# Attention forward: the loads of V are issued from another engine's DMA queue

## The chip, the cores and the metric

The kernel runs on one core of one Trainium2 chip. The metric is the device time of one execution in microseconds (us). A core has a matrix engine (PE; its weight loads are shown as PEld), a vector engine (DVE), a scalar engine (ACT), a general engine (POOL) and a synchronising engine (SP) that here does nothing but issue DMAs. Sixteen DMA engines move data between the device memory and the on-chip buffer.

## The reference

Plain softmax attention over 16 x 32 = 512 heads, each with 192 queries, 1024 keys and a head width of 128, all in bfloat16:

```python
B, H, Sq, Sk, D = 16, 32, 192, 1024, 128

def reference(q, k, v):
    scale = q.shape[-1] ** -0.5
    scores = jnp.einsum("bhqd,bhkd->bhqk", q, k) * scale
    p = _softmax(scores, axis=-1)
    return jnp.einsum("bhqk,bhkd->bhqd", p, v)
```

## The kernel before

**Heads, pairs, units.** Two heads make a pair, and their 2 x 192 query rows are cut into three units of 128 rows: `A` is 128 rows of the first head, `B` 128 rows of the second, and `S` the remaining 64 rows of each. Two pairs, that is four heads with six units (`A0 B0 A1 B1 S0 S1`), make one period; the three order strings at the top of the file say in which order each engine works on a period's units, and a prime in them means "of the period before". Sixteen heads (`G=16`) make a group of 24 units and four periods (`UPG = 24`); there are 32 groups (`NGR`).

**What is done to a unit.** PE multiplies q by the transposed K into PSUM (`qk`, buffer `s_ps`). DVE scales the scores, copies them to the on-chip buffer `ss` and finds the row's extreme (L332). ACT takes the exponential with the row sum (L373), or, for the units called shifted, POOL subtracts the maximum (L207) and ACT takes the exponential later. PE transposes the result (`tr`, buffer `pt_ps`), ACT evacuates that to `pt_sb` (`evac`, L382 and L384), and PE multiplies it by V (`pv`, buffer `o_ps`). DVE divides by the row sums into `ob` (L357). On PE the `pv` products run one period behind the `qk` products, that of `B1` two periods behind, so the last `pv` of a group is the first `pv` in the second period of the next group.

**Loads and stores.** All DMAs are issued by SP, in one order. K and q are loaded by transposing DMAs into `kt` and `qt` (L141, L145), V by a plain DMA into `vs` (L152), in runs of 2048 bytes. Each of the three buffers has two slots (`NS=2`), each holding a whole group, so group g goes into the slot of group g - 2. Group 0 comes in three pieces (`FIRST`), group 1 whole. After that, SP goes through the groups: for each g it loads K and q of g + 2 once all `qk` of g are done (semaphore `s_qk`, L161), loads V of g + 2 once all `pv` of g are done (`s_pv`, L164), and then stores the outputs of g once they are complete (`s_on`, L169). A DMA issue that finds its queue full holds SP until there is room.

**Who waits for V.** PE waits for the V of a group at the group's first `pv` (L313, semaphore `svl`), for q at its first `qk` (L257) and for K right after (L266). ACT's program is one list (`ACT_ORDER`, L20, run at L387):

```python
ACT_ORDER = "exp:B0 exp:A1 ev:A0 ev:B0 exp:S0 ev:A1 exp:S1 ev:B1 ev:S0 ev:S1"
```

Of the kernel before, what the change touches and what calls it, by code (L numbers as in the profile page):

```python
# [12 lines left out]
UNITS = ("A0", "B0", "A1", "B1", "S0", "S1")  # L13
# [9 lines left out]
def _order(text, periods):  # L23
    ops = [(w.split(":")[0], w.split(":")[1].rstrip("'"), w.count("'")) for w in text.split()]
    for p in range(periods + max(back for _, _, back in ops)):
        for op, name, back in ops:
            if 0 <= p - back < periods:
                if name in UNITS:
                    yield op, 6 * (p - back) + UNITS.index(name)
                else:  # L30
                    yield op, 2 * (p - back) + int(name)


def _attention_kernel(nc, q, k, v, out, G=16, NS=2, NSS=5, NX=4, NPT=5,
                      FIRST=((0, 2), (2, 8), (8, 16)), LAST=((0, 4), (4, 6), (6, 7), (7, 8))):
# [5 lines left out]
    NGR = NH // G  # L41
    PPG = G // 2
    UPG = 3 * PPG
    NU = NGR * UPG
    KT_TILES = SK // 128
# [7 lines left out]
    vf = v.rearrange("b h s d -> (b h) s d")  # L53
    of = out.rearrange("b h s d -> (b h) s d")

    def shifted(u):
        return UNITS[u % 6] in SHIFTED
# [12 lines left out]
    with ExitStack() as es:  # L70
        def sb(name, shape, dt):
            return es.enter_context(nc.sbuf_tensor(name, shape, dt))
# [4 lines left out]
        def sem(name):  # L77
            return es.enter_context(nc.semaphore(name))
# [3 lines left out]
        vs = sb("vs", [128, NS, G, KT_TILES, 128], BF16)  # L82
# [15 lines left out]
        svl = [sem("svl%d" % i) for i in range(NS)]  # L98
        sf = [sem("sf%d" % i) for i in range(len(FIRST))]
        sfv = [sem("sfv%d" % i) for i in range(len(FIRST))]  # L100
# [7 lines left out]
        s_pv = sem("s_pv")  # L108
# [5 lines left out]
        def unit_info(u):  # L114
            name = UNITS[u % 6]
            pr = 2 * (u // 6) + int(name[1])
            return pr, "ABS".index(name[0]), pr // PPG, pr % PPG
# [3 lines left out]
        def words(t):  # L121
            return t.rearrange("p t q -> p (t q)").bitcast(F32)
# [10 lines left out]
        def pair_units(pr):  # L133
            return [u for u in range(6 * (pr // 2), 6 * (pr // 2) + 6) if unit_info(u)[0] == pr]

        @block.sync
        def _(e):
            def load_kq(g, a, b, sems):
                s = g % NS
                h0 = g * G  # L140
                e.dma_start_transpose(  # L141
                    kt[:, s, :, a * 128:b * 128],
                    kf[h0 + a:h0 + b].rearrange("g (p t) d -> (g p) (t d)", t=KT_TILES),
                ).then_inc(sems[0], 16)
                e.dma_start_transpose(  # L145
                    qt[:, s, a * SQ:b * SQ],
                    qf[h0 + a:h0 + b].rearrange("g r d -> (g r) d"),
                ).then_inc(sems[1], 16)

            def load_v(g, a, b, sm):  # L150
                h0 = g * G
                e.dma_start(  # L152
                    vs[:, g % NS, a:b],
                    vf[h0 + a:h0 + b].rearrange("g (p t) d -> p g t d", t=KT_TILES),
                ).then_inc(sm, 16)

            def loads(g):
                s = g % NS
                last_u = (g - NS + 1) * UPG - 1
                if g >= NS:  # L160
                    e.wait_ge(s_qk, last_u + 1)  # L161
                load_kq(g, 0, G, (sxk[s], sxq[s]))
                if g >= NS:
                    e.wait_ge(s_pv, last_u + 1)  # L164
                load_v(g, 0, G, svl[s])

            def stores(g, a, b):
                so = g % NSO
                e.wait_ge(s_on, g * PPG + b)  # L169
                e.dma_start(  # L170
                    of[g * G + 2 * a:g * G + 2 * b].rearrange("h r d -> (h r) d").rearrange(
                        "(n p) d -> p n d", p=128),
                    ob[:, so, a:b].rearrange("p pg y d -> p (pg y) d"),
                ).then_inc(sst[so], 16)

            n = len(FIRST)
            for i in range(n):
                load_kq(0, *FIRST[i], (sf[i], sf[i]))
                if i > 0:
                    for i2 in range(i if i > 1 else 0, i + 1):  # L180
                        load_v(0, *FIRST[i2], sfv[i2])
            for g in range(1, min(NS, NGR)):
                loads(g)
            for g in range(NGR):
                if g + NS < NGR:
                    loads(g + NS)
                for a, b in (LAST if g == NGR - 1 else ((0, PPG),)):
                    stores(g, a, b)
            for so in range(min(NSO, NGR)):
                n_uses = len(range(so, NGR, NSO))  # L190
                if so == (NGR - 1) % NSO:
                    n_uses += len(LAST) - 1
                e.wait_ge(sst[so], 16 * n_uses)
# [23 lines left out]
        def _(pe):  # L217
# [19 lines left out]
            def qk(u):  # L237
# [13 lines left out]
                if g == 0:  # L251
                    for i, (h, _) in enumerate(FIRST):
                        if h <= b and i not in seen_kq:
                            seen_kq.add(i)
                            pe.wait_ge(sf[i], 32)
                elif u % UPG == 0:
                    pe.wait_ge(sxq[s], load_cnt(g))  # L257
# [27 lines left out]
            def pv(u):  # L285
# [14 lines left out]
                for t in range(KT_TILES):  # L300
                    first = t == 0
                    last = t == KT_TILES - 1
                    for at, rows, x in tiles:
                        w = PTS[:, t, rows]
                        pe.ldweights(w, tile_position=at)  # L305
                        if first and at[1] == 0:
                            if g == 0:
                                for i, (h, _) in enumerate(FIRST):
                                    if h <= b and i not in seen_v:
                                        seen_v.add(i)  # L310
                                        pe.wait_ge(sfv[i], 16)
                            elif u % UPG == 0:
                                pe.wait_ge(svl[s], load_cnt(g))  # L313
                            if k3 == 0 and pr >= 2:
                                pe.wait_ge(s_on, pr - 1)
                        ins = product(O[rows, sl, :], w, vs[:, s, x, t, :], at, first, last)
                        if with_rs:
                            ins = product(O[rows, 3, sl: sl + 1], w, ones[:, 0:1], at, False, last)
# [49 lines left out]
        @block.scalar  # L368
        def _(act):
            def exp_first(u):  # L370
                act.wait_ge(s_max, u + 1)
                pr, k3, g, pg = unit_info(u)
                act.activation(  # L373
                    x_sb[:, u % NX, :], ss[:, u % NSS, :], ACT_FN.Exp,
                    bias=nb[:, u % NSS: u % NSS + 1], scale=-1.0,
                    accum_out=rs[:, pr % NRS, O_SLOT[k3]: O_SLOT[k3] + 1],
                ).then_inc(s_xa, 1)

            def evac(u):
                act.wait_ge(s_tr, u + 1)  # L380
                if shifted(u):
                    act.activation(pt_sb[:, u % NPT], pt_ps[u % 2][:], ACT_FN.Exp, scale=-1.0).then_inc(s_ev, 1)  # L382
                else:
                    act.activation(words(pt_sb[:, u % NPT]), words(pt_ps[u % 2][:]), ACT_FN.Copy).then_inc(s_ev, 1)  # L384

            do = {"exp": exp_first, "ev": evac}
            for op, u in _order(ACT_ORDER, NU // 6):  # L387
                do[op](u)


def bass_standalone__mha_softmax__near_ridge_kernel(
    nc: bass.Bass,
    q: bass.AP,
    k: bass.AP,
    v: bass.AP,
    out: bass.AP,
):
    _attention_kernel(nc, q, k, v, out)
# [28 lines left out]
```

## Time and profile before

| what | value |
|---|---|
| median of 3 runs | 1204.29 us (1203.57 to 1207.56) |
| profiled execution, its time | 1201.59 us |
| its span, first to last instruction | 1199.9 us |
| granted clock of PE | 0.984 |
| busy PE / DVE / ACT / POOL | 94% / 91% / 90% / 40% |
| PE waits for q | 32.7 us in 12 waits |
| PE waits for V | 29.6 us in 22 waits |
| moved by DMA | 321.25 MB, 268 GB/s on average |
| packets of the DMA queue that the program's own transfers use | 789712, 318.78 MB |
| packets of the instruction queue (queue 8) | 132, 2.16 MB |

The span is the time from the first to the last instruction of the one profiled execution; the run that it was taken from took 1201.59 us, and the median of the timed runs is 2.7 us above that. The page gives each engine's busy time, the span cut into 40 slices with the busy share of each engine and of the DMA engines in tenths (9 is 90% or more), and the chain of work that ended last. A time "to landing" is from a DMA's issue to the arrival of its data. In SP's timeline the length of a row is how long SP was held by that issue, not how long the data took.

The transfers of one group as the trace has them (us from the start of the span; group 15 is in the middle of the run):

| transfer | issued | SP held for | landed |
|---|---|---|---|
| K of group 15 | 536.10 | 25.91 | 566.0 |
| q of group 15 | 562.06 | 4.58 | 568.7 |
| V of group 15 | 566.68 | 0.58 | 581.8 |
| outputs of group 13 | 567.31 | 4.63 | 584.4 |

For the same group, the last `qk` product of group 13, whose slots it takes, ends at 535.9, and the last `pv` product of group 13 at 546.8.

### The profile page before, as it was taken

What the parts mean: (1) busy time and instruction counts of PE and PEld (TensorE: products, weight loads), DVE (VectorE), ACT (ScalarE), POOL (GpSimd) and SP (SyncE); (2) the same over time, 40 slices, a digit from 0 to 9 for tenths busy, and PEclk for the clock granted to TensorE, in tenths of its full rate; (3) what the DMA queues carried; (4) which work ended last, traced back from release to release, by engine and by line L of the source; (5) the groups of instructions that cost most, each with busy time, mean ns of one, the idle gap of its engine ahead of it and who ended that gap; (6) DMA issues with size and microseconds to landing.
All of it is one profiled execution on the core that took longest, in us unless ns stands there. A gap on an engine that the chain in (4) does not pass through costs nothing.

```text
span 1199.9 us, 38792 instructions
## 1 busy us (share of the span) xinstructions
PE 1130.4 (94%) x18432; PEld 849.9 (71%) x15360; DVE 1089.1 (91%) x2304; ACT 1082.9 (90%) x1793; POOL 485.3 (40%) x262
## 2 busy tenths in 40 slices
PE   5699999999999999999999999999999999999998
PEld 3477777777777777677776777777777777777766
DVE  5589899989998999899999999989999899989987
ACT  4689899989998999899998999989999899989988
POOL 2234344434343434344443443434444344334432
PEclk9899999999999999999999999999999999999999
DMA  9999999999999999999999999999999999999991
GB/s 233 244 280 276 284 283 259 262 293 280 284 269 243 282 284 282 278 269 258 287 288 273 286 259 269 290 283 276 270 251 281 289 281 288 259 252 294 284 273 32
DMA packets 789882, 321.25 MB, mean 268 GB/s; under 512 B 724176, under 2 KB 724176, under 8 KB 789712
## 3 DMA queue, kind: packets, MB, share of 16 engines
q1 hardware_dynamic: 789712, 318.78, 112.2%
q8 instruction: 132, 2.16, 0.7%
q14 instruction: 38, 0.31, 0.1%
HBM read 134.22 MB, written 25.17 MB: 133 GB/s over the span
## 4 chain that ended last, share of the span: by engine, by line
PE 62%; DMA 29%; SPq 8%; ACT 2%; issue 0%; DVE 0%
DMA vs<-in_v_dram 28%; PE o_ps L220 22%; PE pt_ps L220 20%; PE s_ps L220 19%; SPq L141 4%; SPq L145 3%; ACT x_sb L373 1%; DMA qt<-in_q_dram 1%; ACT pt_sb L384 0%; ACT pt_sb L382 0%; SPq L152 0%; DVE ob L357 0%; DVE rinv L355 0%
## 5 line engine op out<-in xcount | busy, mean ns | idle before, releaser
L332 DVE TENSOR_SCALAR_CACHE_REDUCE ss<-s_ps 128x1024 f32<-128x1024 f32 x768 | 920.4, 1220 | 94.3 <-PE s_ps L220 76.4
L207 POOL TENSOR_TENSOR x_sb<-ss,nb 128x1024 bf16<-128x1024 f32 x256 | 484.6, 1893 | 702.6 <-DVE ss L332 683.3
L305 PEld LDWEIGHTS <-pt_sb 128*128 128x128 bf16 (+1 forms) x8192 | 443.8, 104 | 232.8 <-issue 135.1
L373 ACT ACTIVATE x_sb<-ss,nb 128x1024 bf16<-128x1024 f32 x512 | 585.3, 1145 | 12.6 <-DVE ss L332 12.6
L220 PE MATMUL o_ps<-vs,pt_sb 128*128 128x128 bf16 (+1 forms) x8192 | 498.1, 219 | 31.8 <-DMA vs<-in_v_dram 29.6
L220 PE MATMUL s_ps<-kt,qt 128*128 128x512 bf16 (+1 forms) x2048 | 468.7, 387 | 33.2 <-DMA qt<-in_q_dram 32.7
L220 PE MATMUL pt_ps<-ident,x_sb 128*128 128x128 bf16 x6144 | 454.5, 221 | 1.3 <-ACT pt_sb L382 1.3
L279 PEld LDWEIGHTS <-x_sb 128*128 128x128 bf16 x6144 | 369.2, 98 | 62.4 <-issue 62.1
L384 ACT ACTIVATE pt_sb<-pt_ps 128x512 f32<-128x512 f32 x512 | 306.0, 598 | 79.3 <-PE pt_ps L220 79.0
L382 ACT ACTIVATE pt_sb<-pt_ps 128x1024 bf16<-128x1024 bf16 x256 | 260.1, 1016 | 19.7 <-PE pt_ps L220 19.6
L220 PE MATMUL o_ps<-ones,pt_sb 128*128 128x1 bf16 x2048 | 190.0, 166 | 0.0
L357 DVE TENSOR_TENSOR ob<-o_ps,rinv 128x384 bf16<-128x384 f32 x256 | 142.7, 557 | 8.8
L263 PEld LDWEIGHTS <-qt 128*128 128x128 bf16 (+1 forms) x1024 | 79.8, 104 | 51.4 <-DMA qt<-in_q_dram 28.3
L373 ACT ACTIVATION_READ_ACCUMULATOR x_sb<-ss,nb 128x1 f32 x512 | 100.7, 197 | 0.0
L332 DVE DVE_READ_ACCUMULATOR ss<-s_ps 128x1 f32 x768 | 63.6, 83 | 0.0
L355 DVE RECIPROCAL rinv<-o_ps 128x1 f32<-128x1 f32 x256 | 41.6, 163 | 4.2 <-PE o_ps L220 4.2
L345 DVE RECIPROCAL rinv<-rs 128x2 f32<-128x2 f32 x256 | 40.9, 160 | 1.1 <-ACT x_sb L373 1.1
L373 ACT ACT_TABLE_LOAD x1 | 1.3, 1283 | 0.8 <-PEq L412 0.8
L199 POOL TENSOR_SCALAR_AFFINE_SELECT ident<-ones 128x128 bf16<-128x128 bf16 x1 | 0.3, 292 | 0.1
L197 POOL MEMSET ones<- 128x128 bf16 x1 | 0.2, 204 | 0.3 <-POOLq L412 0.3
L412 POOL MEMSET const-float32-0.0<- 128x1 f32 x1 | 0.1, 99 | 0.3 <-issue 0.3
L412 POOL MEMSET const-bfloat16-1.0<- 128x1 bf16 x1 | 0.1, 102 | 0.0
(2 smaller groups left out, 0.2 us busy)
## 6 DMA issues: line engine op xcount, KB each, us to landing
vs<-in_v_dram SPq DMA_DIRECT2D x31, 4096.0 KB, 15.2
out_dram<-ob SPq DMA_DIRECT2D x31, 768.0 KB, 17.1
vs<-in_v_dram SPq DMA_DIRECT2D x1, 2048.0 KB, 10.2
vs<-in_v_dram SPq DMA_DIRECT2D x1, 1536.0 KB, 8.8
kt<-in_k_dram SPq DMA_TRANSPOSE x34, 30.4
qt<-in_q_dram SPq DMA_TRANSPOSE x34, 6.1
vs<-in_v_dram SPq DMA_DIRECT2D x1, 512.0 KB, 4.6
out_dram<-ob SPq DMA_DIRECT2D x1, 384.0 KB, 3.2
```

Source lines behind the costliest of these rows:

```text
L141: e.dma_start_transpose(kt[:, s, :, a * 128:b * 128], kf[h0 + a:h0 + b].rearrange("g (p t) d -> (g p) (t d)", t=KT_TILES),).then_inc(sems[ ...
L207: gp.tensor_tensor(x_sb[:, u % NX, :], ss[:, u % NSS, :], nb[:, u % NSS: u % NSS + 1].to_broadcast([128, SK]), ALU.subtract,).then_inc(s_x ...
L220: return pe.add_instruction(mybir.InstMatmult(name=nc.get_next_instruction_name(), engine=mybir.EngineType.PE, ins=[pe.lower_ap(x), pe.low ...
L263: pe.ldweights(w, tile_position=at)
L279: pe.ldweights(w, is_transpose=True, tile_position=(0, 0))
L305: pe.ldweights(w, tile_position=at)
L332: dve.tensor_scalar(ss[:, u % NSS, :], s_ps[u % 2][:].rearrange("p t k -> p (t k)"), -scale, None, ALU.mult, ALU.min, accum_out=nb[:, u % ...
L355: dve.reciprocal(rinv[:, pr % 2, sel], o_ps[pr % 2][:, 3, sel]).then_inc(s_ri, 1)
L357: dve.tensor_tensor(ob[:, so, pg], o_ps[pr % 2][:, 0:3, :], rinv[:, pr % 2, 0:3].unsqueeze(2).to_broadcast([128, 3, 128]), ALU.mult,).then ...
L373: act.activation(x_sb[:, u % NX, :], ss[:, u % NSS, :], ACT_FN.Exp, bias=nb[:, u % NSS: u % NSS + 1], scale=-1.0, accum_out=rs[:, pr % NRS ...
L382: act.activation(pt_sb[:, u % NPT], pt_ps[u % 2][:], ACT_FN.Exp, scale=-1.0).then_inc(s_ev, 1)
L384: act.activation(words(pt_sb[:, u % NPT]), words(pt_ps[u % 2][:]), ACT_FN.Copy).then_inc(s_ev, 1)
```

## The change

Of the V loads, those of groups 0 and 1 stay at SP. Those of groups 2 to 31 are issued by ACT, one DMA of 16 heads for each group as before. ACT issues the load of group g after its evacuation of unit `A1` in the first period of group g - 1, and waits before it until all `pv` of group g - 2 are done, the same count that SP waited for. SP's list for those groups is then K, q, store. Nothing else changes; the helper `load_v` moves out of SP's program and takes the engine as an argument.

```diff
+        def load_v(e, g, a, b, sm):
+            h0 = g * G
+            e.dma_start(
+                vs[:, g % NS, a:b],
+                vf[h0 + a:h0 + b].rearrange("g (p t) d -> p g t d", t=KT_TILES),
+            ).then_inc(sm, 16)
+
         @block.sync
         def _(e):
...
             def loads(g):
                 s = g % NS
                 last_u = (g - NS + 1) * UPG - 1
                 if g >= NS:
                     e.wait_ge(s_qk, last_u + 1)
                 load_kq(g, 0, G, (sxk[s], sxq[s]))
-                if g >= NS:
-                    e.wait_ge(s_pv, last_u + 1)
-                load_v(g, 0, G, svl[s])
+                if g < NS:
+                    load_v(e, g, 0, G, svl[s])
...
             for op, u in _order(ACT_ORDER, NU // 6):
                 do[op](u)
+                g = u // UPG - 1 + NS
+                if op == "ev" and u % UPG == UNITS.index("A1") and NS <= g < NGR:
+                    act.wait_ge(s_pv, (g - NS + 1) * UPG)
+                    load_v(act, g, 0, G, svl[g % NS])
```

More of the change, by code (lines that the diff above doesn't have):

```diff
@@ L148, in load_kq @@
                 ).then_inc(sems[1], 16)
[L150 to L155, printed above, removed]
             def loads(g):
@@ L180, in _ @@
                     for i2 in range(i if i > 1 else 0, i + 1):
-                        load_v(0, *FIRST[i2], sfv[i2])
+                        load_v(e, 0, *FIRST[i2], sfv[i2])
             for g in range(1, min(NS, NGR)):
```

## The prediction, made before the changed kernel was run

> **What bounds the kernel now.** I read the page first (the DMA line, the issues, the chain), then SP's timeline, then rates in short windows.
>
> ```profile
> DMA  9999999999999999999999999999999999999991
> DMA vs<-in_v_dram 28%; PE o_ps L220 22%; PE pt_ps L220 20%; PE s_ps L220 19%; SPq L141 4%; SPq L145 3%; ACT x_sb L373 1%; DMA qt<-in_q_dram 1%; ACT pt_sb L384 0%; ACT pt_sb L382 0%; SPq L152 0%; DVE ob L357 0%; DVE rinv L355 0%
> vs<-in_v_dram SPq DMA_DIRECT2D x31, 4096.0 KB, 15.2
> out_dram<-ob SPq DMA_DIRECT2D x31, 768.0 KB, 17.1
> ```
>
> The DMA engines are at 9 tenths or more in every slice but the last. The largest link of the chain of waits is the landing of V, not compute. SP's own timeline, start, length and instruction, shows why V comes when it does:
>
> ```profile
> 530.87 0.58 SPq L152 DMA_DIRECT2D vs<-in_v_dram  x1
> 531.49 4.56 SPq L170 DMA_DIRECT2D out_dram<-ob  x1
> 536.10 25.91 SPq L141 DMA_TRANSPOSE kt<-in_k_dram  x1
> 562.06 4.58 SPq L145 DMA_TRANSPOSE qt<-in_q_dram  x1
> 566.68 0.58 SPq L152 DMA_DIRECT2D vs<-in_v_dram  x1
> 567.31 4.63 SPq L170 DMA_DIRECT2D out_dram<-ob  x1
> 571.98 27.49 SPq L141 DMA_TRANSPOSE kt<-in_k_dram  x1
> ```
>
> Each row starts where the one above ends (562.06 + 4.58 = 566.64, next 566.68): SP is never held by a semaphore here, only by a queue that is full. From the V issue at 129.68 to that at 1149.38 lie 28 groups, so a group takes 36.42 us. Compute alone is faster. In the chain in order of time the sixteen transposes of one period of four heads come back every 8.64 us, so a group of 16 heads needs 34.56:
>
> ```profile
> 79.30 1.00 PE pt_ps L220 x16
> 87.94 1.00 PE pt_ps L220 x16
> 96.57 1.00 PE pt_ps L220 x16
> 105.21 1.00 PE pt_ps L220 x16
> ```
>
> The difference, 1.86 us a group, is what PE waits for loads: for V 29.6 us in 22 waits and for q 32.7 in 12. Windows (length, busy time of PE, PEld, DVE, ACT and POOL, clock, DMA share, GB/s) give the rates. The first is K alone, the second V alone, the third a hole in the K transposes:
>
> ```profile
> 558.00:560.00 2.00, 2.00 (x48) 1.53 (x43) 1.97 (x4) 1.76 (x3) 0.91 (x1) 1.00 1.28 290
> 570.00:572.00 2.00, 2.00 (x32) 1.38 (x19) 2.00 (x5) 2.00 (x4) 0.00 (x0) 1.00 1.05 404
> 589.20:590.40 1.20, 1.20 (x24) 1.00 (x15) 1.20 (x3) 1.20 (x3) 0.00 (x0) 1.00 0.18 7
> ```
>
> Per group: K 4.19 MB at 290 GB/s is 14.5 us, q 0.79 MB 2.7, V 4.19 MB at 404 is 10.4, and the store 0.79 MB 2.7 at K's rate: 30.3 us. The other 6.1 of 36.42 are such holes and the seams between transfers. Most holes follow an instruction fetch (queue 8, 132 packets of 16 KB): while one DMA engine carries that packet, the transposes of all sixteen stop. So the kernel is paced by DMA work.
>
> **The change, part by part.**
>
> *SP loses 30 V issues* (groups 2 to 31; four stay). They took 0.58 us each, 17 us in all, but SP spends its time blocked on a full queue, so this is worth 0 on the path.
>
> *ACT gains 30 issues and 30 waits.* Each stands after the evacuation of A1 in a group's first period. That evacuation needs its transposes, which PE runs right behind the last probabilities-times-V product of the group before; the semaphore has reached its count by then, so I cost the wait at 0. Behind the issue stand the exp of S1 and then evacuations that PE waits for. The issue is put at 0.58 us, SP's row. It delays ACT, which is busy 3.76 or 4.00 of each 4 us in steady state, about 1.0 us free a group; the 1.86 us of DMA cover stand over that. If both covers were gone: 30 x 0.58 = 17 us. Bounds: 0 to 4.6 us each (a direct transfer issued behind a backlog, the store rows above); I take 0.58, the same instruction, hence 0 on the path.
>
> *V's transfer moves.* Now it is issued some 20 us after it could be: group 13's last V product ends at 546.8, and V(15), which takes its slot, is issued at 566.68. Afterwards it starts about 1 to 2 us after that product and shares the engines with K(g) of the same group. V was late and becomes early; K and q, which shared with nobody, become late. That is no exchange at par, since q opens a group's compute and V is wanted only 11 us later (q product first done at 537.5, V product first done at 548.1).
>
> Following it from the start: K(2) is issued at 58.70 and q(2) lands at 95.0, V(2) behind it at 106.9. Afterwards V(2) is issued at about 76 (group 0's last V product ends at 74.3) and its 10.4 to 11.9 us go ahead of the rest of K(2) and q(2), so q(2) lands at about 106. From there each period carries the same list, K, q, V, store, and stays saturated. At the end V(31) landed last, at 1164.9, and q(31) at 1152.9; now q(31) is last, at about 1164.9, a delay of 12.0. What follows q(31) was 1199.9 - 1152.9 = 47.0 us, in it about 1 us of waiting for V, which goes. Sum: +12 - 1 = +11 us. I also stepped through it with the pieces K 18.3, q 3.3, V 11.3, store 3.5 (the 30.3 with the 6.1 spread over them) and compute of 34.56: this gives 1200.1 for the kernel before (trace 1199.9) and 1210.8 with V and K sharing evenly.
>
> The Trainium skill (DMA: Bandwidth & Descriptors, "Queues, rings and completion order") says that an engine takes turns between queues packet by packet. V's 2048-byte packets take 84 ns in the trace and K's 256-byte ones 14 (1134 a us over 16), so by that rule V would get six sevenths, and the same stepping gives 1212.3. Nothing in the sum rests on it.
>
> *What two queues do to the rate* the trace does not show in bulk. From below: the holes fill and the period falls to compute's 34.56, -1.86 x 29 = -54 us. From above: each group gets another pair of seams like those seen where transposes end and V starts (0.87 us lost) and where the store ends and K starts (0.75), 1.6 x 29 = +47. The nearest row is the fetch, a plain packet from another queue amid transposes: it takes 960 ns there against 1053 within V, so passing costs it nothing, and within a V stretch it costs the others 0.11 us. I take 0.1 a group, +3 us.
>
> The Trainium skill (same page, "Issuing engines are not separate DMA queues") says that a second issuing engine saves only the issue time, since all run on the same 16 DMA engines. The rows agree that issue is not what is short. By it the rate term would be 0 and the sum +11.
>
> Sum: +11 + 3 = +14 on the profiled span of 1199.9 (its run took 1201.59). The median shown is 1204.29, 2.7 above that run; I add the same 14: **1218**.
>
> **The rivals.**
>
> *The holes fill (faster).* Place: K's holes. A fetch that falls into K costs 0.97 us of the next 1.5, one of queue 14 0.66: 83 and 25 of them, 97 us, 3.2 a group. If V flows on the idle engines during them, half of it is 1.6 x 29 = 46, less the 11: 1204 - 35 = 1169; capped by compute it is 1204 - 54 + 11 = 1161. It decides from 0.38 us a group on (11 / 29). For it: sixteen engines do stand idle. Against: at 562.80 an 8 KB packet of queue 14 came while the transposes were about to stop, and took 1679 ns instead of 309, ending with the hole; a plain packet behind stuck transposes seems to be stuck too.
>
> *New seams (slower by more).* The 1.6 us a group above: 1204 + 11 + 47 = 1262. For it: transposes stop on all engines when one is late, and V makes them uneven. Against: the fetch's own time. A milder form: V gets little, a quarter of the engines, lands after it is wanted, and the stepping gives +24: 1228.
>
> *ACT is held.* If the issue takes the store's 4.6 us: 4.6 - 1.86 - 1.0 = 1.7 a group, 49, and the first q(2) 7 later: 1260. Against: V's issue at SP stayed at 0.58 with K and q queued ahead of it.
>
> *Nothing moves.* The one-time delay is recovered because the list is no longer saturated: 1204. Against: the DMA line.
>
> **How the numbers follow.** Forecast 0.48 (own range 1208 to 1228), holes fill 0.20, new seams or a small share 0.17, ACT held 0.09, nothing 0.06. The range 1175 to 1270 leaves out half of the faster case and the tail of the slow ones, about 0.17. A measurement tells 0.3%, 3.6 us, from no change. Faster is the first rival with a bit of the fourth: 0.21; same 0.07; slower 0.72.
>
> **What would show it.** Right: DMA still at 9 in every slice; V issued some 20 us earlier against its product and PE's waits for V gone; waits for q and K in its place, with q(2) landing near 106 and the last q near 1165; a period still within 0.3 us of 36.4; the issue at ACT near 0.6 us. Wrong: windows in which K and V together move clearly more, or less, than the 30.3 us account says; holes that V fills; ACT idle behind its issue; a period near 34.6 or above 37.

## The result, and the profile after

The changed kernel takes 1281.05 us (1273.52 to 1283.61) against 1203.99, a ratio of 1.062 [1.057, 1.067]. The forecast was 1218 with a range up to 1270: the direction was right, the time lies 11 us above the range. The profiled execution has a span of 1281.9 against 1199.9, 82.0 us more.

The page of the changed kernel: the DMA engines by slices, the chain of waits by line, and the DMA issues with their time to landing.

```profile
DMA  9999999999999999999999999999999999999962
PE o_ps L219 24%; PE s_ps L219 23%; PE pt_ps L219 22%; DMA qt<-in_q_dram 22%; SPq L148 6%; DMA vs<-in_v_dram 1%; SPq L152 1%; ACT x_sb L372 0%; SPq L138 0%; ACT pt_sb L383 0%; ACT pt_sb L381 0%; DVE ob L356 0%; DVE rinv L354 0%
vs<-in_v_dram ACTq DMA_DIRECT2D x30, 4096.0 KB, 23.3
kt<-in_k_dram SPq DMA_TRANSPOSE x34, 36.6
qt<-in_q_dram SPq DMA_TRANSPOSE x34, 8.5
```

The engines have packets in flight for 9 tenths of nearly every slice, as before, but that counts packets that stand still too: they move 251 GB/s on average against 268. V, 28% of the chain before, is 1% now; q, 1% before, is 22%. K now lands 36.6 us after its issue (30.4 before), q after 8.5 (6.1), V after 23.3 (15.2). What PE waited for, in us, times and longest, in the changed kernel:

```profile
PE s_ps L219 <- DMA qt<-in_q_dram: 123.9, 31, 10.1
PE o_ps L219 <- DMA vs<-in_v_dram: 1.0, 1, 1.0
```

The waits for V (29.6) are gone, those for q have grown from 32.7 to 123.9. ACT's own price is not among them. Its timeline around one V issue:

```profile
587.54 0.59 ACT L383 ACTIVATE pt_sb<-pt_ps 128x512 f32<-128x512 f32 x1
588.02 1.15 ACT L372 ACTIVATE x_sb<-ss,nb 128x1024 bf16<-128x1024 f32 x1
588.35 0.38 ACTq L138 DMA_DIRECT2D vs<-in_v_dram  x1
```

The issue takes 0.38 us and lies under an exponential of 1.15.

**Where the 82 us are.** I take the time at which the first product of a group with q is done. For group 2 it moved from 98.0 to 109.7: +11.7, once. From group 2 to group 31 a group takes 38.87 us in place of 36.40: 29 x 2.47 = +71.6. From there to the end 44.9 in place of 46.2: -1.3. Together 82.0. (The product times that the text before the result gives for groups 0, 13 and 14 are one product too late: the last products of group 13 end at 534.5 and 545.2, about 1.5 us earlier, and the last V product of group 0 at 71.3, 3 us earlier. The distances that were used, 11 us and some 20, stand.)

So the price is a rate. It is not PE's clock: the granted clock is 0.953 against 0.984, but PE's waits for q are 4.0 us a group (123.9 in 31), and with the 34.56 of compute they make 38.6 of the 38.87. Windows of the changed kernel (length, busy times, clock, DMA share, GB/s): K alone; K and V together; a hole after an instruction fetch while V and K alternate; the start of V:

```profile
586.00:588.00 2.00, 2.00 (x37) 1.65 (x26) 2.00 (x4) 2.00 (x4) 0.30 (x1) 1.00 1.28 290
602.00:604.00 2.00, 2.00 (x43) 1.41 (x35) 1.97 (x5) 2.00 (x5) 1.57 (x1) 1.00 1.07 388
605.80:606.80 1.00, 1.00 (x23) 0.90 (x14) 0.93 (x4) 1.00 (x3) 0.82 (x1) 1.00 1.34 46
595.00:596.50 1.50, 1.50 (x29) 1.15 (x17) 1.50 (x3) 1.50 (x4) 0.00 (x0) 1.00 0.70 49
```

Together the two queues move 388 GB/s, no more than V alone (404 before), and between 604 and 605 us of the span the trace has 175 packets of V and 175 of K, as many of one as of the other. A packet of V has 2048 bytes and one of K 256, so in this stretch V gets eight ninths of what is moved. The Trainium skill (DMA: Bandwidth & Descriptors, "Queues, rings and completion order") has engines take turns by packets; these equal counts agree.

The loss lies in the holes. I counted packets in slices of 0.1 us, called 1134 small packets or 196 of V a us full speed, and summed what is missing, for groups 5 to 29:

| kernel | us a group | lost a group |
|---|---|---|
| before | 36.44 | 6.13 |
| changed | 38.83 | 8.52 |

Both differ by 2.39. That has to be so, since each group moves the same packets and the period less the loss is 30.3 in both; what the count adds is the place of the loss. In the kernel before, holes with a fetch cost 3.81 us a group, all of them among K, q and outputs; within V, counted as holes, they cost 0.01. In the changed kernel they cost 2.67 there and 2.55 while V and K alternate, 5.22 in all. A 16 KB fetch during V cost 0.11 of the next 1.5 us before, and costs 0.80 now. The seams, where one kind of transfer gives way to another (transposes to V; in the changed kernel also V back to transposes), cost 0.97 before and 2.0 now. So of the 2.39, fetches account for 1.41 and seams for 1.03.

### The profile page after: what moved, and what is told of

The parts are those of the page before. It is cut to its first block, busy times and chain, and to the rows that moved or that the text cites. A ratio compares the mean times of both kernels' runs of the same rounds, so it can differ in the third digit from the quotient of the medians.

```text
span 1281.9 us, 38792 instructions
## 1 busy us (share of the span) xinstructions
PE 1151.8 (90%) x18432; PEld 863.2 (67%) x15360; DVE 1088.6 (85%) x2304; ACT 1084.4 (85%) x1793; POOL 485.3 (38%) x262
## 4 chain that ended last, share of the span: by engine, by line
PE 69%; DMA 23%; SPq 7%; ACT 1%; issue 0%; DVE 0%
PE o_ps L219 24%; PE s_ps L219 23%; PE pt_ps L219 22%; DMA qt<-in_q_dram 22%; SPq L148 6%; DMA vs<-in_v_dram 1%; SPq L152 1%; ACT x_sb L372 0%; SPq L138 0%; ACT pt_sb L383 0%; ACT pt_sb L381 0%; DVE ob L356 0%; DVE rinv L354 0%
## 5 line engine op out<-in xcount | busy, mean ns | idle before, releaser
L304 PEld LDWEIGHTS <-pt_sb 128*128 128x128 bf16 (+1 forms) x8192 | 452.2, 105 | 208.4 <-issue 112.7
L219 PE MATMUL s_ps<-kt,qt 128*128 128x512 bf16 (+1 forms) x2048 | 479.0, 392 | 124.5 <-DMA qt<-in_q_dram 123.9
L219 PE MATMUL o_ps<-vs,pt_sb 128*128 128x128 bf16 (+1 forms) x8192 | 507.1, 220 | 1.1 <-DMA vs<-in_v_dram 1.0
L219 PE MATMUL pt_ps<-ident,x_sb 128*128 128x128 bf16 x6144 | 459.6, 222 | 1.3 <-ACT pt_sb L381 1.3
L219 PE MATMUL o_ps<-ones,pt_sb 128*128 128x1 bf16 x2048 | 200.1, 170 | 0.0
## 6 DMA issues: line engine op xcount, KB each, us to landing
vs<-in_v_dram ACTq DMA_DIRECT2D x30, 4096.0 KB, 23.3
kt<-in_k_dram SPq DMA_TRANSPOSE x34, 36.6
```

What stands on the lines that cost most here:

```text
L219: return pe.add_instruction(mybir.InstMatmult(name=nc.get_next_instruction_name(), engine=mybir.EngineType.PE, ins=[pe.lower_ap(x), pe.low ...
```

## The experiments

Times are compared with the kernel before on the same chip, whose median was 1199 to 1204.

**V early, but in one queue.** K in two parts, V between them, all at SP; and as control the same cut with V behind q:

```diff
...
+                load_k(g, 0, 12, sxk[s])
+                e.wait_ge(s_pv, last_u + 1)
                 load_v(g, 0, G, svl[s])
+                load_k(g, 12, G, sxk[s])
+                load_q(g, 0, G, sxq[s])
...
```

> V is back in SP's queue, put where it now arrives: after the K of 12 heads, ahead of the K of the last 4 and of q. The order of the data is that of the changed kernel, the packets of V and K do not alternate. If alternating packets cost the 2.4 us a group (38.83 against 36.44), the period returns to 36.4 to 36.9 and only the one-time delay of q stays: 1204 + 11 to 25, 1215 to 1230. If the order costs it (K of the next group waits for its slot with nothing but a store to cover it), the period stays at 38.5 or more and the time at 1270 to 1285.

> Control for the run above: K in two transposes of 12 and 4 heads, V behind q at SP as in the kernel before. Both theories: within 5 us of 1204. Above 1215 the cut of K itself has a price, which is then taken off the run above.

Measured: 1266.41, 1.051 [1.047, 1.056]; control 1213.50, 1.007 [1.004, 1.010]. SP's timeline of the first:

```profile
527.78 14.20 SPq L144 DMA_TRANSPOSE kt<-in_k_dram  x1
542.02 1.54 SPq L163 DMA_DIRECT2D vs<-in_v_dram  x1
543.61 15.92 SPq L144 DMA_TRANSPOSE kt<-in_k_dram  x1
559.57 4.18 SPq L152 DMA_TRANSPOSE qt<-in_q_dram  x1
563.80 0.58 SPq L185 DMA_DIRECT2D out_dram<-ob  x1
```

Much of such a price comes without any second queue. A group takes 38.10 us against 36.79 in the control: 1.31 for V's place alone, more than half of the 2.47. SP is hardly held by K's slot: the rows follow one another, and over the whole run the issue of K waits 7.0 us in all, 15.5 in the changed kernel. So the theory that K waits for its slot falls; lost time a group is 7.82 against 6.55, and the seam where V gives way to K, which the control does not have, accounts for 1.40. That does not divide the 2.47 of the changed kernel: there V's packets alternate with K's, and its own count has 1.03 on seams and 1.41 on fetches. What this pair shows is that a V in the middle of K has a price of this size without any second queue.

**V in two pieces in one queue.** K in 10, 3 and 3 heads, half of V in each gap.

```diff
...
+                load_k(g, 0, 10, sxk[s])
+                e.wait_ge(s_pv, last_u + 1)
+                load_v(g, 0, 8, svl[s])
+                load_k(g, 10, 13, sxk[s])
+                load_v(g, 8, G, svl[s])
+                load_k(g, 13, G, sxk[s])
+                load_q(g, 0, G, sxq[s])
...
```

> As the run with V between two parts of K in SP's queue, but K in 10, 3 and 3 heads and V in two halves between them: one more place where V follows K and one more where K follows V. If each such pair of seams costs some 1.3 us a group, and each cut of K 0.4, the period rises from 38.1 to 39.5 to 40 and the time from 1266 to 1305 to 1320. If it was the early place of V, not the seams: V is no earlier than there, 1266 to 1280.

Measured 1336.44, 1.114 [1.112, 1.116]; 40.53 us a group. A second cut adds 2.4 us, more than the seam theory's 1.3 and the 0.4 for a cut of K, so its size was too small and its direction right. V's bytes did not change and the place of its first half only by two heads of K; what changed most is the number of seams.

**Half of V on each queue.**

```diff
...
-                    load_v(act, g, 0, G, svl[g % NS])
+                    load_v(act, g, 0, G // 2, svl[g % NS])
...
```

with the other 8 heads from SP behind q.

> 8 heads of V from ACT as in the changed kernel, the other 8 from SP behind q as before. Alternating packets: half of the 2.4 us a group, period 37.6, and half of the one-time delay: 1204 + 35 + 6 = 1245, 1235 to 1255. Order (K waiting for its slot with too little cover): 2 MB of V, 5.2 us, lie between q and the next K again, so nearly all of it goes: 1210 to 1220.

Measured 1321.51, 1.096 [1.092, 1.099]: worse than all of V on ACT, against both theories, 40.42 us a group. Half the alternating packets did not halve the loss. What did grow is the number of places where V enters: once among K and once behind q, with 9.83 us lost a group. This fits seams, not packets.

**More instruction fetches**, in the kernel before and in the changed one: 32 empty instructions after each subtraction on POOL.

```diff
...
                 ).then_inc(s_xp, 1)
+                for _ in range(32):
+                    gp.engine_nop()
...
```

> The kernel before with 32 empty instructions after each subtraction on POOL, which has time for them: 256 more instructions a group, one instruction fetch of 16 KB more a group, 32 in all. Fetches stop all transposes for some 1.26 us and hardly touch V alone: two thirds of them fall into K, 32 x 0.84 = 27, 1225 to 1235. If the holes only happen to stand beside fetches, or POOL's instructions matter in another way: 1200 to 1210.

> The same 32 empty instructions in the changed kernel. If V that alternates with K no longer shelters a fetch, each costs its 1.2 us wherever it falls: 32 x 1.2 = 38, 1281 + 38 = 1319, 1312 to 1326, so more than the 27 of the kernel before. If V shelters as before: 1281 + 27 = 1308.

Measured: 1211.38, 1.010 [1.007, 1.013], and 1295.04, 1.080 [1.078, 1.082]. The instructions came as 64 more packets of 8 KB on queue 14, not as 32 of 16 KB. More fetches do slow the kernel, about 12 us in the kernel before and, taking 1.080 less 1.062, about 21 in the changed one. The second is larger as expected, but 1.062 is known to half a per cent only, so 15 to 28 us is possible against 9 to 15: that V shelters fetches less when it alternates with K rests on the counts in the trace, and this pair does not settle it.

**V from ACT, but later.** The unit named in the condition moves the issue: the third period after A1, its end after S1, the second period after A1.

```diff
-                if op == "ev" and u % UPG == UNITS.index("A1") and NS <= g < NGR:
+                if op == "ev" and u % UPG == 12 + UNITS.index("A1") and NS <= g < NGR:
```

> V stays in ACT's queue, but is issued in the third period of a group instead of the first, some 17 us later, when most of K and q of that group have passed. If alternating packets cost the time, little is left to alternate with: 1204 to 1225, period below 37.2. If the second queue as such is slow, or costs ACT time, nothing is gained: 1275 to 1290. If the order with an early V was the cost, V behind q gives 1204 to 1215.

> V from ACT some 3.5 us later than in the third-period run, after the evacuation of S1, without a wait for q. If the price of the second queue lies in V entering among K and q of its own group, V now comes behind them in nearly every group: 1195 to 1215, with less scatter than 1199 to 1244. If V now runs into K of the next group instead and splits it: 1230 to 1290.

> V from ACT in the second period, halfway between the changed kernel (1281) and the run with the third period (1229). By seams and alternating packets V still enters in the middle of K or just ahead of q, so as many seams as in the changed kernel, and q is late by all of V: 1265 to 1300. If the loss shrinks in step with how late V enters: 1250 to 1260.

Measured: third period 1229.05, but from 1199.14 to 1243.60, too scattered for an interval; its end 1299.75, 1.081 [1.078, 1.085]; second period 1190.51, 0.990 [0.983, 0.997]. None of the three medians lies in a range that I expected, and the price does not fall steadily the later V comes. At the end of the third period V is issued about 2 us before K of the next group and runs into it. There it also comes too late, and PE waits for it 98.2 us (29.6 in the kernel before, 1.0 in the changed one), so this time is not the price of a split K alone:

```profile
PE o_ps L219 <- DMA vs<-in_v_dram: 98.2, 30, 4.6
```

In the second period it meets the end of q: 5.49 us lost a group, less than the 6.13 of the kernel before, and the seam in front of V, 0.97 there, down to 0.4. So the second queue as such is not slow.

Two neighbours of it, after B1 and after S1 of the second period:

> V from ACT in the second period, after the evacuation of B1, some 1.7 us later than the run that took 1190 against 1200. If V is best where it enters with the end of q, so that neither K nor q is cut and V starts without a hole (lost per group 5.5 us there, 6.1 in the kernel before, 8.5 in the changed one): fewer packets of q alternate with V, 0.98 to 0.99 of the kernel before, 1176 to 1190. If that run was a lucky phase: 1200 to 1250.

> The same after the evacuation of S1, some 3.5 us later than the first. By the end-of-q theory V now follows q or just meets its last packets: 0.975 to 0.99, 1170 to 1188. If the gain needs V to overlap q's end, part of it is lost again and some groups fall into the bad case seen in the third period (V just ahead of a late q): 1195 to 1230.

Measured 1200.26, 1.003 [1.000, 1.005], and 1202.96, 1.003 [1.000, 1.005]. Neither expected gain came. The trace of the first says why: of its 29 steps from group 2 on, 17 are 34.5 us, the time of compute alone, and five are 39.6 to 41.5 (steps are from one group's first product with q to the next's). The first of these, from SP's and then ACT's timeline:

```profile
212.75 23.33 SPq L148 DMA_TRANSPOSE kt<-in_k_dram  x1
236.12 14.12 SPq L152 DMA_TRANSPOSE qt<-in_q_dram  x1
250.29 0.58 SPq L169 DMA_DIRECT2D out_dram<-ob  x1
```

```profile
234.91 0.37 ACTq L138 DMA_DIRECT2D vs<-in_v_dram  x1
```

V is issued at 234.91, q only at 236.12 and then it is held for 14.12 us, against 3.98 in the next group. In a good group of the same run V follows q:

```profile
559.39 3.92 SPq L152 DMA_TRANSPOSE qt<-in_q_dram  x1
```

```profile
561.81 0.37 ACTq L138 DMA_DIRECT2D vs<-in_v_dram  x1
```

In the first case V has overtaken q, and q is held some 10 us longer, about the time of V.

**V held until it cannot overtake.** ACT waits before the issue; first for q, in the third period, then for K, in the second:

```diff
...
+                    act.wait_ge(sxk[g % NS], load_cnt(g))
                     load_v(act, g, 0, G, svl[g % NS])
```

> V from ACT in the third period, but ACT first waits until q of that group has landed, so V never alternates with q or K of its own group; ACT is held for it when q is late. In the run without this wait a V issued just before q (497.1 against 497.3) made q take 13.7 us to issue and its group 12 us longer. If that was what scattered its times (1199 to 1244): 1180 to 1205, with little scatter. If ACT's wait costs more: 1215 to 1240.

> V from ACT in the second period after the evacuation of S1, and ACT first waits until K of that group has landed, so only packets of q and the store can alternate with V, and V never stands ahead of q. Overtaking theory: the slips of 40 to 43 us (six in the run without the wait) go, also the one of the first group (44.8 to about 37), steps of 34.5 to 35.5: 98 + 29 x 35 + 45 = 1158, 1155 to 1180. Theory of two queues as such: 1195 to 1210 as before.

> The same, 1.7 us earlier, after the evacuation of B1: ACT is held by K more often. Overtaking theory: 1155 to 1185, some us above the run after S1 if ACT's holding matters. Two queues as such: 1195 to 1210.

> The run with V after A1 of the second period once more, unchanged: 0.985 to 0.995 if its gain is real, 1.00 if it was the phase of those runs.

Measured: waiting for q 1240.92, 1.034 [1.033, 1.036]; for K after S1 1196.41, 0.996 [0.995, 0.998]; for K after B1 1188.23, 0.990 [0.988, 0.993]; the second period after A1 once more 1189.78, 0.990 [0.988, 0.992]. With the wait after B1 no step from group 2 on exceeds 37.5 us: the slips are gone, which the overtaking theory asked for and the theory of two queues did not. After S1 three steps of 38.2 to 40.1 are left, and the time lies in the range that the theory of two queues gave, 1195 to 1210; the run after B1 lies below it. The times that the overtaking theory gave, 1155 to 1185, were missed by both: the wait moves part of the price to ACT. In the run after B1:

```profile
ACT pt_sb L383 <- DMA kt<-in_k_dram: 37.0, 16, 5.6
PE s_ps L219 <- DMA qt<-in_q_dram: 25.2, 4, 10.7
```

ACT stands 37.0 us for K, and the waits for q fall from 123.9 in the changed kernel to 25.2. And SP's queue runs empty: in its timeline the output's issue ends at 523.51 and K follows only at 533.61, when its slot is free, while V passes. In this run that gap stands in every group, some 10 us; in the kernel before there was none.

```profile
518.63 4.26 SPq L152 DMA_TRANSPOSE qt<-in_q_dram  x1
522.93 0.58 SPq L169 DMA_DIRECT2D out_dram<-ob  x1
533.61 22.08 SPq L148 DMA_TRANSPOSE kt<-in_k_dram  x1
```

Waiting for q in the third period is later than either: ACT was held there too, V then met K of the next group, and 7.38 us were lost a group.

Two versions thus beat the kernel before by about 1%, and the changed one by more: V from ACT after A1 of the second period, which still has such slips in some groups, and the one after B1 that waits for K.

## Why the prediction was right and wrong

*Right.* The kernel is paced by DMA work: PE's waits for V went from 29.6 to 1.0 us, and the time rose all the same. The wait on ACT cost nothing; the issue took 0.38 us (0.58 assumed) and was hidden. That V early makes q late was the centre of the forecast: q of group 2 landed at 108.5 (about 106 forecast), and the delay of the first groups was 11.7 us (12.0). The end of the span lost 1.3 us (1). These terms, put at +11, measured +10.4. They are an eighth of the 82 us, so the direction came out right for a small part of what made it.

*Wrong.* The step that failed is "What two queues do to the rate", where I took 0.1 us a group, +3 us; it measured 2.47 a group, +71.6. Its upper bound of 1.6 was too low as well, and so the range was. A period above 37, named as a sign of being wrong, is what came. Two things were wrong in it. I went by the fetch's own time, 960 ns within K against 1053 within V, and concluded that passing costs nothing; but that row tells what a plain packet suffers from the transposes, and the question was what transposes and V suffer together. The answer stood in a row that I used for another rival: a fetch within K cost 0.97 of the next 1.5 us and within V 0.11. That shelter, a third of the period, is lost when V alternates with K; this part rests on the trace, not on a run of its own. And the seams, which I had as a bound and gave 0.17, were paid in each run that put V into the middle of K: 1.31 us a group with one queue, and 1.03 more than before by the count in the changed kernel.

*The rivals.* "New seams" gave 1262 and comes nearest; that a V among K's transposes is paid for is shown by the runs with one queue, which reach 1266 without ACT; that the changed kernel pays it in the same place is not shown. Its milder form, a quarter of the engines for V, did not happen: V got as many packets as K, and landed in 23 us. "The holes fill" did not happen: in the mixed stretch a hole stops V too (46 GB/s). "ACT is held" is ruled out by the issue of 0.38 us and the missing wait, "nothing moves" by the period.

*Open.* How the 2.47 us divide between seams and lost shelter rests on the counts in one trace: no run takes away one without the other, and the runs with more fetches point to the shelter only within their error. Why a second cut of K cost 2.4 and not 1.7 stays open too.

## What to carry to other kernels

In a kernel paced by transfers, ask of a load that is moved earlier what it now stands in front of: here V gained 20 us that nobody needed, and q, which opens the next group, paid. Keep a plain load out of the middle of a run of transposes, and let it start where they end; here that place, not the queue, was worth 7% with V issued by ACT both times (1.062 in the changed kernel, 0.990 in the second period). And where two queues feed the same engines, the load that is issued first can take the engines first, as V did here by 1.2 us, so tie the load that may not overtake to the one that must be first.

## What the hardware showed that was not expected

A V that enters among transposes was paid for by the entry rather than by its size: with half of V on each queue 3.70 us a group more were lost than in the kernel before (9.83 against 6.13), with all of it on ACT 2.39 more. An instruction fetch of 16 KB, a single packet, stops nearly all transposes (7 GB/s in the hole against 290) and, when V alternates with them, V too: 46 GB/s against 388. Between V's issue at 588.35 and its first packet, at 593.9, 5.6 us passed although its queue was empty, while the K issued before it went on; over the 30 issues, all made while SP was held by its issue of K, it was 4.3 to 6.2 us. In the run with V at the end of the third period, where SP had nothing to issue at that time, it was 1.0 to 1.1 us in all 30.
